# Attention and a routed expert layer in one program: routing sums in the accumulator's own bank, expert weights asked for before rows, pads written one at a time

## The chip, the cores and the metric

The program runs on one core of one Trainium2 chip. The metric is the device time in microseconds (us) of one execution; of several executions the median is taken. Five engines work side by side, each through its own instructions in order: PE (matmuls), DVE (vector work), ACT (activations), POOL (here mostly scatters by DMA) and SP (which issues most of the DMAs). They wait for each other through semaphores. PE writes its results into PSUM, eight banks of which this kernel uses all.

## What is computed

The reference has two halves. The first, for each of 8 batches of 2496 tokens with 256 channels:

```python
scores = scale * np.matmul(z, z.transpose(0, 2, 1))
attn = np.maximum(scores, 0.0) ** 2
out = np.matmul(attn, v)
return (u * out).astype(np.float32)
```

The second takes these 19968 rows x, and sends each row to the one of 8 experts with the largest logit:

```python
xn = x / (np.linalg.norm(x, axis=-1, keepdims=True) + 1e-06)
logits = xn @ en.T / tau
expert_idx = np.argmax(logits, axis=1)
...
h = np.maximum(x[mask] @ w1[e], 0.0)
out[mask] = gate_w[mask, None] * (h @ w2[e])
```

Here gate_w is the softmax value of the chosen expert.

## The kernel before, in words

**Attention.** Each batch is cut into 5 groups of up to 512 tokens, and each group runs over 20 steps of 128 tokens: 800 steps in all, one after the other. In a step PE computes a block of scores (L300, L301), ACT takes relu and square (L303, L307), DVE splits the square into a high and a low half in 16 bits (L314, L315), and PE multiplies the halves with the values into two accumulators, `acc[0]` and `acc[1]` (L344 to L346, in the last step of a group L341 and L342). Scores are symmetric, so a block below the diagonal is not computed again but taken from an earlier one, turned by DMA; steps that make their own block are called own steps here. Halves are made four own steps ahead of their use, scores five. In the first step of a group the matmuls into `acc[1]` are held back into the second step.

**PSUM.** Three banks hold scores (psS). Four hold accumulators (psA): two for the group at work, two for the group before it. One bank (psM, tile `pm`) is shared by everything small: the sum of squares of a group (`total`, L383), its logits (`logits`, L412), the ranks of its rows within the experts (`rank`, L496), and the scales of weights, z and v (L131, L147, L553, L571). While one user's result lies in `pm`, the next user waits. A flag, `state["pm"]`, and the third entry of a queue item keep the pieces of weight preparation from being started into an occupied `pm` (`pm_free`).

**Routing.** When a group's last step is done, `route` puts its pieces into a queue, each with the number of steps after which it is due: gate_x 0 (DVE: accumulators times u, L374), squares 4 (ACT, L378), total 7 (PE, L383), scale 9 (DVE, L391), high 11 (ACT, L398), low 13 (DVE, L401), turn 15 (SP, four turning DMAs, L406), logits 17 (PE), take 19 (DVE, L431, L432), top 20, rank 23 (PE), place 25 (DVE, L506 to L515: row positions, from `pm`), and from 34 to 48 the norm and the gates; scatters 49 (POOL, L521) write the rows into the table xs in DRAM, sorted by expert. The pieces of a group so run during the next two groups or so. Group numbers below count through all batches, from 0 to 39. The order of ACT, DVE and SP is that of the program text; PE and POOL are ordered by a planner of the framework, which can put a small matmul some steps later if it thinks its input late.

**Experts.** Rows are taken from xs in 61 tiles of 256 and 41 of 128 (slots). A slot loads rows (`slot_x`: a turning DMA, L890, and the gates, L891), weights (`slot_w`, up to 1 MB each, L904; from the fifth slot on only if the expert changes, L906), does the first layer (`slot_up`: tiles `ph` in psA, L923 to L925, relu on ACT L927, low half on DVE L928) and the second (`slot_down`, L947 to L949, DVE L953), and scatters the results (POOL, L954). Rows are asked for six slots ahead, weights four. The pieces still in the queue go on during the first slots: `pop` advances the step count by one after each tile. `slot_first` asks for the first slots' rows and weights during the last group, at step 789; it stands in SP's order behind the scatters of group 36. A read of xs waits for all scatters before it in the program, a scatter for the reads before it.

**Pads.** Behind the last row of each expert a block of 128 rows with an invalid index is written into xs (L861), at a position that SP reads from a table. All eight are written by one queue item, `pads`, due after the last group's scatters and the final table.

Of the kernel before, what the change touches and what calls it, by code (L numbers as in the profile page):

```python
# [7 lines left out]
F32 = mybir.dt.float32  # L8
F32R = mybir.dt.float32r
F16 = mybir.dt.float16  # L10
BF16 = mybir.dt.bfloat16
I32 = mybir.dt.int32
# [7 lines left out]
P = 128  # L20
# [8 lines left out]
TABLE = 36  # L29
NWB = 4  # L30
XFIRST, XAHEAD = 3, 6


def ceil_div(a, b):
    return -(-a // b)
# [10 lines left out]
def relu2_attention_then_moe(ctx, tc, zT, uT, v, emb, tau, w1, w2, ident, tri, iota_e, out):  # L46
    nc = tc.nc
    B, DQ, S = zT.shape
    D = uT.shape[1]
    E, _, F = w1.shape  # L50
# [25 lines left out]
    psM = ctx.enter_context(tc.tile_pool(name="psM", bufs=1, space=PSUM))  # L76
# [212 lines left out]
    state = {"pm": False}  # L289
# [66 lines left out]
    def route(b, g, acc, ut):  # L356

        t0, n = groups[g]
        nj = ceil_div(n, P)
# [10 lines left out]
        loc = {}  # L370
# [8 lines left out]
            loc["ssq"] = ssq  # L379

        def total():
            pm = psM.tile([P, 512], F32, name="pm", tag="m")
            nc.tensor.matmul(pm[:, 0:1], ones_b, loc["ssq"].bitcast(BF16)[:, 1:2], start=True, stop=True)  # L383
            loc["pm"] = pm
            state["pm"] = True

        def scale():
            pm = loc.pop("pm")
            state["pm"] = False
            h = rt.tile([P, 1], I32, name="h23", tag="h23")  # L390
            nc.vector.tensor_scalar(h, pm.bitcast(I32)[:, 0:1], 24, 23,  # L391
                                    op0=ALU.logical_shift_right, op1=ALU.logical_shift_left)
            up = rt.tile([P, 1], F32, name="up", tag="up")
            nc.vector.tensor_scalar(up.bitcast(I32), h, -1.0, float(198 << 23), op0=ALU.mult, op1=ALU.add)
            loc.update(h=h, up=up)
# [10 lines left out]
                nc.sync.dma_start_transpose(row16[:, 0:nj, q * P:(q + 1) * P], xhl[:, q, 0:nj * P])  # L406

        def logits():
            pm = psM.tile([P, 512], F32, name="pm", tag="m")
            for j in range(nj):  # L410
                for q in range(4):
                    nc.tensor.matmul(pm[:, j * 2 * E:(j + 1) * 2 * E], xhl[:, q, j * P:(j + 1) * P], enhl[:, q % 2, :],  # L412
                                     start=(q == 0), stop=(q == 3))
            loc["pm"] = pm
            state["pm"] = True

        def rest_scale():
            h, up = loc["h"], loc["up"]
# [6 lines left out]
            loc.update(odn=odn, epu=epu)  # L425

        def take():
            pm = loc.pop("pm")
            state["pm"] = False
            pv = pm[:, 0:nj * 2 * E].rearrange("p (j c) -> p j c", c=2 * E)  # L430
            nc.vector.tensor_copy(lg[:, :nj, :], pv[:, :, 0:E])  # L431
            nc.vector.tensor_tensor(lg[:, :nj, :], lg[:, :nj, :], pv[:, :, E:], op=ALU.add)  # L432
            m = rt.tile([P, 4], F32, name="m", tag="m")
            nc.vector.tensor_reduce(m[:, :nj], lg[:, :nj, :], axis=AX.X, op=ALU.max)
            sh = rt.tile([P, 4, E], F32, name="sh", tag="sh")
            nc.vector.tensor_tensor(sh[:, :nj, :], lg[:, :nj, :], m[:, :nj].unsqueeze(2).broadcast_to([P, nj, E]), op=ALU.subtract)
            loc["sh"] = sh
# [80 lines left out]
        def scatters():  # L518
            for j in range(nj):
# [2 lines left out]
                    xs[:, :], bass.IndirectOffsetOnAxis(ap=loc["dsti"][:m, j:j + 1], axis=0),  # L522
                    row[:m, j, 0:ROW], None)

        return [(0, gate_x), (4, squares), (7, total, True), (9, scale), (11, high), (13, low), (15, turn), (17, logits, True),
                (18, rest_scale), (19, take), (20, top), (23, rank, True), (25, place), (34, sums)] \
            + [(36 + j, norm(j)) for j in range(nj)] \
            + [(41, root), (42, roots), (43, shifted), (46, exps), (48, gates), (49, scatters)]
# [93 lines left out]
    steps = [(b, g, s) for b in range(B) for g in range(NG) for s in range(NST)]  # L622
# [42 lines left out]
    ones_b = cst.tile([P, P], BF16, name="ones_b")  # L665
# [58 lines left out]
    pm = psM.tile([P, 512], F32, name="pm", tag="m")  # L724
# [130 lines left out]
    nc.vector.memset(pad.bitcast(I32)[:, D + 1:D + 2], N)  # L855
    tails = cst.tile([1, E], I32, name="tails")

    def pads():
        for e in range(E):
            r = nc.sync.value_load(tails[0:1, e:e + 1], min_val=e * CAP, max_val=e * CAP + N)  # L860
            nc.sync.dma_start(xs[bass.ds(r, TB), :], pad[:TB])  # L861

    nc.sync.dma_start(xs[E * CAP:E * CAP + TB, :], pad[:TB])

# [2 lines left out]
    queue = []  # L867
# [9 lines left out]
    def slot_of(k):  # L877
        return (tables["A"], k, TA) if k < KA else (tables["B"], k - KA, TB)

    def slot_x(k):  # L880

        tab, i, T = slot_of(k)
        off = nc.sync.value_load(tab[0:1, 0, i:i + 1], min_val=0, max_val=E * CAP + TB - T)
        if k < XFIRST:
            xt = mx.tile([P, 4, T], F16, name="xt16", tag="xt16")
            me = mx.tile([P, T // P, ROW - D], F32, name="me", tag="me")
        else:
            xt = mst["mr"].tile([P, 4, T], F16, name="xr16", tag="xr16")
            me = mst["mr"].tile([P, T // P, ROW - D], F32, name="mer", tag="mer")
        nc.sync.dma_start_transpose(xt, xs[bass.ds(off, T), :].bitcast(F16)[:, 0:2 * D])  # L890
        nc.sync.dma_start(me, xs[bass.ds(off, T), D:ROW].rearrange("(j p) w -> p j w", p=P))  # L891
        mst["x", k] = xt, me

    def slot_w(k, i):
        tab, c, _ = slot_of(k)
        if i == 0:
            e = nc.sync.value_load(tab[0:1, 1, c:c + 1], min_val=0, max_val=E - 1)
            new = None if k < NWB else nc.sync.value_load(tab[0:1, 2, c:c + 1], min_val=0, max_val=1)
            mst["e", k] = e, new
        else:  # L900
            e, new = mst.pop(("e", k))
        src = wsd[bass.ds(e, 1), :, (0, WR1)[i]:(WR1, WR1 + WR2)[i]].rearrange("e p w -> (e p) w")
        if new is None:
            nc.sync.dma_start(mst["w"][i][k], src)  # L904
        else:
            nc.sync.dma_start(mst["w"][i][k % NWB], src, cond=new, cond_hint=False)  # L906
# [52 lines left out]
    def slot_first():  # L959

        mst["w"] = ([wp.tile([P, WR1], F16, name="wa0", tag="wr1"), wp.tile([P, WR1], F16, name="wa1", tag="wo")],
                    [wp.tile([P, WR2], F16, name="wb0", tag="wr2")])
        slot_x(0)
        slot_w(0, 0)
        slot_w(0, 1)
        slot_w(1, 0)
        for k in range(1, XFIRST):
            slot_x(k)

    def slot_pools():  # L970
# [48 lines left out]
    for i, (b, g, s) in enumerate(steps):  # L1019
# [49 lines left out]
        if i == len(steps) - 1 - NST // 2:  # L1069
            for f in follow:  # L1070
                if f is not None:
                    f()
            follow = []
            slot_weights()
            slot_first()
        if s == NST - 1:
            queue += [(i + p[0], p[1], len(p) > 2) for p in route(b, g, accs.pop((b, g)), uts.pop((b, g)))]
            if b == B - 2 and g == NG - 1:
                queue.append((i + TABLE, table_a, False))
            queue.sort(key=lambda x: x[0])  # L1080
            run(i)
        if own:
            if nd + LOOK - 1 < len(direct):
                st = direct[nd + LOOK - 1]
                halves[st] = parts(*st, probs.pop(st))
            nd += 1
    queue += [(len(steps) + TABLE, table_b, False), (len(steps) + TABLE, pads, False)]
    state["step"] = len(steps) - 1
    actx.close()
    slot_pools()  # L1090
# [102 lines left out]
```

## Time and profile before

| | us |
|---|---|
| median of 3 executions | 2218.98 (2212.02 to 2219.06) |
| the profiled execution | 2217.79 |
| its span, first to last instruction | 2215.6 |
| mean granted TensorE clock, share of full | 0.988 |
| PE busy | 2105.5 (95%) |
| DVE busy | 1421.2 (64%) |
| ACT busy | 1197.7 (54%) |
| POOL busy | 349.9 (16%) |

Attention lasts to about 1348 us of the span, the experts from there to the end. Times in the timeline are us from the span's start. "Idle before" is the time in which the engine had nothing to do before an instruction, and the arrow names what ended it; the releaser is inferred from semaphores. SPq is SP's queue of DMA issues: such a row tells when the DMA was issued, not when it landed.

### The profile page before, as it was taken

The page shows a single profiled execution, that of the slowest core. Times are in us where ns is not written, and L with a number is a line of the kernel's source. Part 1 is how long each engine was busy: PE and PEld are TensorE (multiplying, and loading weights), DVE is VectorE, ACT ScalarE, POOL GpSimd, SP SyncE. Part 2 cuts the span into 40 slices and gives each one's busy share as a digit, 9 for nine tenths or more (in the row PEclk, how much of TensorE's full clock was granted, in tenths as well). Part 3 has the DMA queues.
Part 4 walks back from the last instruction along what each step waited for, and adds up shares of the span by engine and source line. Part 5 has one row for each costly group of instructions (what it writes and reads, how often), then busy time and mean ns, then how long its engine had stood idle before and what let it go on. Part 6 is the DMA issues. An engine that isn't in the chain of part 4 may idle for free. (4 is left out here: it accounts for less than half of the span.)

```text
span 2215.6 us, 43233 instructions
## 1 busy us (share of the span) xinstructions
PE 2105.5 (95%) x15154; PEld 1345.1 (61%) x15154; DVE 1421.2 (64%) x3796; ACT 1197.7 (54%) x2329; POOL 349.9 (16%) x428
## 2 busy tenths in 40 slices
PE   6999899999999989999999998999999999999997
PEld 2444444444444434444444446888888888889996
DVE  7778878889888878788988864443333333333332
ACT  6768768768868758768868762222222222222221
POOL 0011111111111111111111111221111111111211
PEclk9999999999999999999999999999999999999999
DMA  6756957885975955967966646442233332237460
GB/s 167 174 129 186 203 149 183 189 209 137 209 195 140 234 138 132 248 151 185 207 178 148 138 98 204 112 122 62 56 89 87 91 93 49 50 101 196 107 165 27
DMA packets 610316, 317.85 MB, mean 143 GB/s; under 512 B 530981, under 2 KB 573486, under 8 KB 602928
## 3 DMA queue, kind: packets, MB, share of 16 engines
q1 hardware_dynamic: 594912, 273.82, 52.7%
q0 software_dynamic: 15184, 41.24, 5.8%
q8 instruction: 121, 1.98, 0.4%
q14 instruction: 99, 0.81, 0.1%
HBM read 297.95 MB, written 59.60 MB: 161 GB/s over the span
## 5 line engine op out<-in xcount | busy, mean ns | idle before, releaser
L303 ACT ACTIVATE a<-sc 128x512 f32<-128x512 f32 (+1 forms) x480 | 278.1, 580 | 109.3 <-PE sc L301 105.8
L307 ACT ACTIVATE a<-a 128x512 f32<-128x512 f32 (+1 forms) x480 | 300.6, 626 | 15.1
L346 PEld LDWEIGHTS <-vv 128*128 128x128 f16 x1520 | 149.4, 98 | 179.4 <-issue 11.2
L947 PE MATMUL po<-w,hh 128*128 128x256 f16 x944 | 257.3, 273 | 0.0
L949 PE MATMUL po<-w,hl 128*128 128x256 f16 x944 | 257.3, 273 | 0.0
L948 PE MATMUL po<-w,hh 128*128 128x256 f16 x944 | 257.3, 273 | 0.0
L344 PEld LDWEIGHTS <-vv 128*128 128x128 f16 x1520 | 149.3, 98 | 176.2 <-ACT vv L281 8.0
L521 POOL DMA_INDIRECT xs<-row,dsti x160 | 176.3, 1102 | 505.2 <-DMA xs<-row,dsti 296.2
L345 PEld LDWEIGHTS <-vv 128*128 128x128 f16 x1520 | 149.4, 98 | 164.5 <-issue 5.1
L954 POOL DMA_INDIRECT out_dram<-ot,mer x153 | 148.8, 972 | 608.8 <-DVE ot L953 374.5
L344 PE MATMUL acc<-tt,vv 128*128 128x512 f16 (+1 forms) x640 | 238.7, 373 | 1.1 <-DMA tt<-hl__372 1.1
L346 PE MATMUL acc<-tt,vv 128*128 128x512 f16 (+1 forms) x640 | 238.9, 373 | 0.0
L345 PE MATMUL acc<-tt,vv 128*128 128x512 f16 (+1 forms) x640 | 238.8, 373 | 0.0
L300 PE MATMUL sc<-z 128*128 128x512 f16 (+1 forms) x480 | 183.1, 382 | 11.6 <-ACT a L303 6.6
L953 DVE TENSOR_SCALAR ot<-po,mer,w 128x256 f32<-128x256 f32 x114 | 58.0, 541 | 200.1 <-PE po L949 194.8
L301 PE MATMUL sc<-z,z 128*128 128x512 f16 (+1 forms) x480 | 183.0, 381 | 0.0
L949 PEld LDWEIGHTS <-hl 128*128 128x128 f16 x1272 | 124.5, 98 | 14.5
L947 PEld LDWEIGHTS <-hh 128*128 128x128 f16 x1272 | 124.5, 98 | 13.9
L948 PEld LDWEIGHTS <-hh 128*128 128x128 f16 x1272 | 124.5, 98 | 13.9
L449 POOL MEMSET ob<- 128x72 bf16 x40 | 6.2, 158 | 664.7 <-DVE pos L511 645.9
L947 PE MATMUL po<-wb,hh 128*128 128x256 f16 x328 | 89.4, 273 | 0.0
L949 PE MATMUL po<-wb,hl 128*128 128x256 f16 x328 | 89.4, 273 | 0.0
(4162 smaller groups left out, 5148.1 us busy)
## 6 DMA issues: line engine op xcount, KB each, us to landing
w<-wsd SPq DMA_DIRECT2D x73, 1026.0 KB
wa<-wsd SPq DMA_DIRECT2D x50, 1024.0 KB
w<-wsd SPq DMA_DIRECT2D x48, 1024.0 KB
wb<-wsd SPq DMA_DIRECT2D x25, 1026.0 KB
scan<-in_v_dram SPq DMA_DIRECT2D x56, 312.0 KB
vt<-in_v_dram SPq DMA_DIRECT2D x133, 128.0 KB
ut<-in_uT_dram SPq DMA_DIRECT2D x32, 512.0 KB
wr<-in_w_dram SPq DMA_DIRECT2D x16, 1024.0 KB
```

The source lines that it names most:

```text
L300: nc.tensor.matmul(sc[:, :n], z1[:, ss], z1[:, t0:t0 + n], start=True, stop=False)
L301: nc.tensor.matmul(sc[:, :n], z1[:, ss], z2[:, t0:t0 + n], start=False, stop=True)
L303: nc.scalar.activation(a[:, :n], sc[:, :n], AF.Relu, scale=2.0 ** -SHIFT)
L307: nc.scalar.activation(a[:, :n], a[:, :n], AF.Square)
L344: nc.tensor.matmul(acc[k][:, :n], va, ph[:, :n], start=first, stop=False)
L345: nc.tensor.matmul(acc[k][:, :n], va, pl[:, :n], start=False, stop=False)
L346: nc.tensor.matmul(acc[k][:, :n], vb, ph[:, :n], start=False, stop=last)
L521: nc.gpsimd.indirect_dma_start(xs[:, :], bass.IndirectOffsetOnAxis(ap=loc["dsti"][:m, j:j + 1], axis=0), row[:m, j, 0:ROW], None)
L947: nc.tensor.matmul(o, hh[:, f, t], wh, start=(f == 0), stop=False)
L948: nc.tensor.matmul(o, hh[:, f, t], wl, start=False, stop=False)
L949: nc.tensor.matmul(o, hl[:, f, t], wh, start=False, stop=(f == NF - 1))
L954: nc.gpsimd.indirect_dma_start(out, bass.IndirectOffsetOnAxis(ap=me.bitcast(U32)[:, j, 1:2], axis=0), ot[:, j, :], None, bounds_check=N - ...
```

## The change

`total` and `logits` no longer take a tile of the shared bank. They write into `acc[1]` of their own group, whose contents `gate_x` has read by then; `scale` and `take` read from there. Their queue items lose the mark that keeps others out of `pm`. In `slot_first` the row load of the first slot moves behind the three first weight loads. The eight pads become eight queue items, due 18, 20, ... 32 steps after the table's due time in place of all at once.

```diff
--- before.py
+++ after.py
@@ -379,16 +379,11 @@
             loc["ssq"] = ssq
 
         def total():
-            pm = psM.tile([P, 512], F32, name="pm", tag="m")
-            nc.tensor.matmul(pm[:, 0:1], ones_b, loc["ssq"].bitcast(BF16)[:, 1:2], start=True, stop=True)
-            loc["pm"] = pm
-            state["pm"] = True
+            nc.tensor.matmul(acc[1][:, 0:1], ones_b, loc["ssq"].bitcast(BF16)[:, 1:2], start=True, stop=True)
 
         def scale():
-            pm = loc.pop("pm")
-            state["pm"] = False
             h = rt.tile([P, 1], I32, name="h23", tag="h23")
-            nc.vector.tensor_scalar(h, pm.bitcast(I32)[:, 0:1], 24, 23,
+            nc.vector.tensor_scalar(h, acc[1].bitcast(I32)[:, 0:1], 24, 23,
                                     op0=ALU.logical_shift_right, op1=ALU.logical_shift_left)
             up = rt.tile([P, 1], F32, name="up", tag="up")
             nc.vector.tensor_scalar(up.bitcast(I32), h, -1.0, float(198 << 23), op0=ALU.mult, op1=ALU.add)
@@ -406,13 +401,11 @@
                 nc.sync.dma_start_transpose(row16[:, 0:nj, q * P:(q + 1) * P], xhl[:, q, 0:nj * P])
 
         def logits():
-            pm = psM.tile([P, 512], F32, name="pm", tag="m")
+            pm = acc[1]
             for j in range(nj):
                 for q in range(4):
                     nc.tensor.matmul(pm[:, j * 2 * E:(j + 1) * 2 * E], xhl[:, q, j * P:(j + 1) * P], enhl[:, q % 2, :],
                                      start=(q == 0), stop=(q == 3))
-            loc["pm"] = pm
-            state["pm"] = True
 
         def rest_scale():
             h, up = loc["h"], loc["up"]
@@ -425,9 +418,7 @@
             loc.update(odn=odn, epu=epu)
 
         def take():
-            pm = loc.pop("pm")
-            state["pm"] = False
-            pv = pm[:, 0:nj * 2 * E].rearrange("p (j c) -> p j c", c=2 * E)
+            pv = acc[1][:, 0:nj * 2 * E].rearrange("p (j c) -> p j c", c=2 * E)
             nc.vector.tensor_copy(lg[:, :nj, :], pv[:, :, 0:E])
             nc.vector.tensor_tensor(lg[:, :nj, :], lg[:, :nj, :], pv[:, :, E:], op=ALU.add)
             m = rt.tile([P, 4], F32, name="m", tag="m")
@@ -522,7 +513,7 @@
                     xs[:, :], bass.IndirectOffsetOnAxis(ap=loc["dsti"][:m, j:j + 1], axis=0),
                     row[:m, j, 0:ROW], None)
 
-        return [(0, gate_x), (4, squares), (7, total, True), (9, scale), (11, high), (13, low), (15, turn), (17, logits, True),
+        return [(0, gate_x), (4, squares), (7, total), (9, scale), (11, high), (13, low), (15, turn), (17, logits),
                 (18, rest_scale), (19, take), (20, top), (23, rank, True), (25, place), (34, sums)] \
             + [(36 + j, norm(j)) for j in range(nj)] \
             + [(41, root), (42, roots), (43, shifted), (46, exps), (48, gates), (49, scatters)]
@@ -855,10 +846,11 @@
     nc.vector.memset(pad.bitcast(I32)[:, D + 1:D + 2], N)
     tails = cst.tile([1, E], I32, name="tails")
 
-    def pads():
-        for e in range(E):
+    def pads(e):
+        def f():
             r = nc.sync.value_load(tails[0:1, e:e + 1], min_val=e * CAP, max_val=e * CAP + N)
             nc.sync.dma_start(xs[bass.ds(r, TB), :], pad[:TB])
+        return f
 
     nc.sync.dma_start(xs[E * CAP:E * CAP + TB, :], pad[:TB])
 
@@ -960,11 +952,10 @@
 
         mst["w"] = ([wp.tile([P, WR1], F16, name="wa0", tag="wr1"), wp.tile([P, WR1], F16, name="wa1", tag="wo")],
                     [wp.tile([P, WR2], F16, name="wb0", tag="wr2")])
-        slot_x(0)
         slot_w(0, 0)
         slot_w(0, 1)
         slot_w(1, 0)
-        for k in range(1, XFIRST):
+        for k in range(XFIRST):
             slot_x(k)
 
     def slot_pools():
@@ -1084,7 +1075,7 @@
                 st = direct[nd + LOOK - 1]
                 halves[st] = parts(*st, probs.pop(st))
             nd += 1
-    queue += [(len(steps) + TABLE, table_b, False), (len(steps) + TABLE, pads, False)]
+    queue += [(len(steps) + TABLE, table_b, False), *[(len(steps) + TABLE + 18 + 2 * e, pads(e), False) for e in range(E)]]
     state["step"] = len(steps) - 1
     actx.close()
     slot_pools()
```

## Rows read from the trace of the kernel before

**Rows 1.** The page: span; busy time (us) of each engine.

```profile
span 2215.6 us, 43233 instructions
PE 2105.5 (95%) x15154; PEld 1345.1 (61%) x15154; DVE 1421.2 (64%) x3796; ACT 1197.7 (54%) x2329; POOL 349.9 (16%) x428
```

**Rows 2.** Windows: stretch, length, busy of PE, PEld, DVE, ACT, POOL; clock, DMA, GB/s.

```profile
60.00:1348.00 1288.00, 1223.53 (x6451) 568.15 (x6449) 1056.90 (x3087) 960.72 (x1910) 182.08 (x244) 0.99 0.72 171
1348.00:2204.00 856.00, 841.49 (x8548) 761.60 (x8547) 321.53 (x599) 195.40 (x340) 166.45 (x174) 0.99 0.39 103
...
80.00:120.00 40.00, 34.38 (x167) 15.05 (x166) 26.23 (x60) 20.67 (x36) 0.16 (x1) 0.91 0.85 193
1320.00:1360.00 40.00, 35.41 (x226) 19.99 (x224) 17.91 (x72) 11.26 (x29) 4.57 (x6) 0.91 0.45 130
1480.00:1520.00 40.00, 36.28 (x317) 31.91 (x318) 12.95 (x21) 8.10 (x14) 8.74 (x9) 0.96 0.42 107
```

**Rows 3.** Waits of PE, 60 to 1348 us: total us, times, longest us.

```profile
PE pm L383 <- DVE pos L511: 37.2, 15, 7.0
PE sc L300 <- ACT a L303: 6.6, 10, 1.5
PE pm L553 <- DVE lg L432: 2.6, 2, 1.9
```

**Rows 4.** Timeline of PE: start us, us, instruction, idle before it and releaser.

```profile
113.77 0.16 PE L383 MATMUL pm<-ssq,ones_b 128*128 128x1 bf16 x1 [5.62 <-DVE pos L511]
```

**Rows 5.** Timeline of DVE around the same instant.

```profile
112.65 0.80 DVE L114 TENSOR_REDUCE smxv<-scan 128x1 f32<-128x624 f32 x1 [6.65 <-DMA scan<-in_v_dram]
116.27 0.43 DVE L314 CAST hl__1093<-a 128x512 f16<-128x512 f32 x1
```

**Rows 6.** Timeline of PE, group 18: its sum, then its logits.

```profile
679.09 0.16 PE L383 MATMUL pm<-ssq,ones_b 128*128 128x1 bf16 x1 [2.48 <-DVE pos L511]
...
690.07 0.55 PE L412 MATMUL pm<-enhl,xhl 128*128 128x16 f16 x16
```

**Rows 7.** Timeline of DVE, group 18: the low halves for these logits.

```profile
688.16 1.28 DVE L401 SCALAR_TENSOR_TENSOR xhl<-xt,up,xhl 128x1024 f16<-128x1024 f32 x1
```

**Rows 8.** Timeline of PE: first matmul into the second accumulator, groups 22 and 25.

```profile
769.55 0.38 PE L344 MATMUL acc<-tt,vv 128*128 128x512 f16 x1
...
870.66 0.38 PE L344 MATMUL acc<-hl__10506,vv 128*128 128x512 f16 x1
```

**Rows 9.** Timeline of DVE: last read of the logits, groups 20 and 23.

```profile
765.29 0.19 DVE L432 TENSOR_TENSOR lg<-lg,pm 128x32 f32<-128x32 f32 x1
...
871.91 0.19 DVE L432 TENSOR_TENSOR lg<-lg,pm 128x32 f32<-128x32 f32 x1
```

**Rows 10.** Waits of SP's queue, whole span.

```profile
SPq L890 <- DMA xs<-row,dsti: 42.8, 3, 18.0
```

**Rows 11.** Timeline of SP's queue: first expert rows, first expert weights.

```profile
1344.86 1.27 SPq L890 DMA_TRANSPOSE xt<-xs  x1
...
1347.59 0.36 SPq L904 DMA_DIRECT2D wa<-wsd  x1
```

**Rows 12.** Waits of PE from 1348 us on.

```profile
PE ph__17184 L923 <- DMA wa<-wsd: 4.6, 1, 4.6
PE ph__19315 L923 <- DMA wa<-wsd: 3.8, 1, 3.8
```

**Rows 13.** Timeline of POOL: first scatter of group 36.

```profile
1332.68 0.97 POOL L521 DMA_INDIRECT xs<-row,dsti  x1 [1.76 <-DVE row L489]
```

**Rows 14.** Windows: the three first weight loads in flight.

```profile
1347.00:1359.00 12.00, 7.41 (x40) 4.94 (x38) 3.04 (x10) 1.19 (x2) 0.00 (x0) 0.72 0.96 307
```

**Rows 15.** Waits of POOL, whole span.

```profile
POOL xs L521 <- DMA xs<-row,dsti: 296.2, 106, 7.5
```

**Rows 16.** Timeline of SP's queue: the eight pads.

```profile
1473.63 8.25 SPq L861 DMA_DIRECT2D xs<-pad  x8
```

**Rows 17.** Timeline of ACT after the hand-over: the squares of group 39.

```profile
1366.17 0.95 ACT L378 ACTIVATE xhl<-xt 128x896 f16<-128x896 f32 x1 [4.50 <-DMA row<-xhl]
```

## The prediction

> **What bounds the kernel now.** I read the page first: PE is busy 2105.5 of 2215.6 us, so time can only come out of the 110 us in which it stands still, or out of its clock [rows 1]. The windows by stage say where that is: attention leaves PE idle for 1288.0 - 1223.5 = 64.5 us between 60 and 1348 us, the experts for 14.5 us of 856; the rest is start-up, which the change doesn't touch. In both stages the granted clock averages 0.99, and the short windows show where it falls: behind a wait of some us it drops from its upper level (2.4 GHz) to the lower one (1.2 GHz) for a while, which in a window of 40 us reads as 0.91 or 0.96, a loss of 3.6 or 1.6 us of work on top of the wait [rows 2]. Then the waits of PE: in attention one line holds more than half of the idle time, the sum of squares L383, 37.2 us in 15 waits, released by the previous group's `place` on DVE, which empties the shared bank. Waits on scores are 6.6 us; a transpose for the weights' scales, which waits for `take` to empty the bank, has 2.6 us [rows 3]. From 1348 us on two waits for weights are left, 4.6 and 3.8 us [rows 12].
>
> **Part 1, the accumulator's bank.** Nothing is added: the same matmuls and DVE reads go to another bank. Removed is the wait for `place`; the sum now waits only for its own input. Its worth lies between nothing (PE stands still a little later, for the same DVE) and 37.2 us plus some 10 us of clock. It has two kinds of waits.
>
> Two are long, 5.6 and 7.0 us together 12.6. In the first DVE is itself late: it stood 6.65 us for a scan's DMA, in front of `place`, and the next halves come out at 116.27 us, 2.5 us after PE was let go [rows 4, 5]. PE can bring forward only what was fed to it: I take two steps. A step is 1288/760 = 1.7 us, so 3.4 us for each, 7 in both.
>
> Thirteen are short, 24.6 us, 1.9 on average. Seven of them lie in the fourth group of a batch. In group 18 PE waited 2.48 us; ten us later its logits start at 690.07, and the low halves they need were ready at 688.16 + 1.28 = 689.44: only 0.6 us of the 2.48 can be kept, the rest becomes a wait for `low` [rows 6, 7]. I take 0.6 of each, 8 us. Of the waits of other small work on this bank I take 2 [rows 3].
>
> Added is a new wait. `acc[1]` comes free after `take`, 19 steps into the route, no longer after `gate_x` at 0, and the next user of the bank starts two groups on, some three steps behind `take`. Queued behind it on PE is everything; ACT, and DVE through it, wait for its scores. In the trace PE's first matmul into `acc[1]` of group 22 comes 4.1 us after the last read of group 20's logits; in group 25 it comes 1.4 us before group 23's [rows 8, 9]. Of 38 such pairs seven are short, by 3.9 us together, the rest have up to 5.4 us. I take 4 us. If DVE came later still this bound has no floor but the planner, which can put other matmuls first; as the lower end I take all that the edit saves and 9 more. Part 1: 7 + 8 + 2 - 4 = 13 us, between -9 and 50. The clock I leave at 0, because short waits stay where DVE is late.
>
> **Part 2, weights before rows.** SP stands 18.0 us at the first row load, until group 36's scatters have landed, and asks for the first weights 2.7 us after it; PE then waits 4.6 us for them, and its clock falls [rows 10, 11, 12, 2]. Moved are the row load's table read, turning DMA and gate DMA, past three weight loads of 1 MB on SP's queue. The weights need nothing that is late, so they are asked for at the place where SP now stands still. Rows of the first slot are then last. They can't come before 1344.86 plus their landing, and attention ends near 1348: the saving is between 0 and 4.6 + 3.6 = 8.2 us. The first of four scatters starts at 1332.68, while the weights would still be under way (three took most of the 12 us from 1347 on, with DMA 96% busy at 307 GB/s) [rows 13, 14]. A scatter waits for the one before it, 2.8 us as a rule (296.2 over 106) and 7.5 at worst [rows 15]. Two delayed by a good us each push the rows back by 3. I take 5 of the 8.2.
>
> The Trainium skill (DMA: Bandwidth & Descriptors, section Issuing engines are not separate DMA queues) says that DMAs of SP and POOL run on the same 16 engines and interleave, whoever issued them. By that the scatters do pay for the weights, which speaks against this part; the third rival below is what it would come to here. That scatters under load take up to 7.5 us agrees with it.
>
> Behind the first rows on SP stand the rows of slots 1 and 2 and then the four turning DMAs of group 38. With the weights out of the way they are issued some 3 us earlier, and the squares of group 39, which ACT does only at 1366.17 after 4.5 us of waiting for these DMAs, move forward with them [rows 17]. Against that `acc[1]` of the last group now stays taken through the first four slots, so the expert tiles turn over three banks instead of four. A bank comes free when DVE has read it; normally that is in time, but the fifth tile is held up by these squares, and the eighth would want its bank about 3 us early. I set the two against each other at 0, between -4 and +1.
>
> **Part 3, the pads.** SP writes eight in 8.25 us, one a us, and before that stands for the last scatters; the weights behind them are late and PE waits 3.8 us, then runs for a while at the lower clock, 1.6 us [rows 16, 12, 2]. After the change no pad stands before these weights. The next row load stops SP for the same scatters, but it is one slot later in the program, and rows are asked for six slots ahead, of 856/81.5 = 10.5 us each. Each pad still costs its table read and its DMA, about 1 us, and the wait for the row loads before it; the row load after it waits for its landing. Three pads come to one slot: some 3 us of issues and as much waiting, inside 10.5. What hides that is the lead of four slots for weights. Without it the 3.8 us would come back. I take 5 of 5.4, between 0 and 5.4.
>
> **The sum.** 13 + 5 + 0 + 5 = 23 us off the profiled execution of 2217.8, that is 2194.8. The median of the runs lies 1.2 us above that execution, so 2196.
>
> **Rivals.** First, DVE simply remains the feeder: every wait taken from the sum comes back at the logits, the halves or the new bank wait, and part 1 is worth 2 instead of 13. For it: group 18 above, and DVE is busy 1056.9 of 1288 us in attention. Against: DVE too stands still for 231 us there, partly for what a waiting PE has not made. Time 2207. Chance 0.20.
>
> Second, the buffer does its work: with more lead PE rides over DVE's late stretches, which is what a lead is for, and most of the 37.2 us and 5 us of clock go. Part 1 is then 35, the time 2174. Against it speak the short distances of rows 6 to 9. Chance 0.14.
>
> Third, the scatters pay in full: four at 2 us more each put the first rows back by 8, part 2 gives nothing, time 2201. Chance 0.12.
>
> Fourth, slower: the wait for `take` becomes the new stop of every group. It decides when DVE is later against PE than now by more than the distance of a pair, some 2 us on average. To lose 7 us over all, these waits must eat the 10 of parts 2 and 3 and 17 more, on top of the 37.2 that they replace: 54 us over 38 groups, 1.4 us each, as in group 25. Seven pairs are at or past that point now, and 31 are not. Time 2226. Chance 0.05.
>
> Fifth, the change doesn't do what it says: the sum waits just as long for its squares on ACT, or the planner places it as before, and the weights still come late. The releaser named in the rows is DVE's `place` in all 15 waits, so it has little. Time 2219. Chance 0.04.
>
> **The numbers.** My forecast has 0.45. About 0.3% of this kernel, 6.7 us, is what a measurement of it can tell from no change, so faster means under 2212.3. Forecast, second and third rival lie clear of it, the first near it, and I give a quarter of that to "same": 0.45 + 0.14 + 0.12 + 0.15 = 0.86, of which I move 0.05 to the others for what I have not seen. Faster 0.81, same 0.12, slower 0.07. The range reaches from the second rival, 2174, to the edge of the first, 2213.
>
> **What would show it.** Right: L383 gone from PE's waits on DVE in attention, a smaller wait at the logits (L412) or at the first matmuls into `acc` (L344, released by L432) in its place; the first weights asked for near 1327 us, and PE's first expert matmul released by the rows; no wait of PE near 1484 us and eight pads apart from each other on SP. PE's idle time between 60 and 1348 us should fall from 64.5 to about 50. Wrong: idle time there unchanged, with L344 named instead of L383, or the first rows landing 5 us or more later after the scatters.

## The result, and the profile after

The changed kernel takes 2195.06 us (median of four runs, 2193.44 to 2195.83) against 2219.02 for the kernel before (median of four, measured with it): ratio 0.9895, 95% interval 0.9871 to 0.992. Its profiled execution took 2194.44 us, 23.4 less than the profiled execution before. In the changed kernel the lines have moved up: the sum of squares is L382, the logits L407, `take`'s last read L423, `place` ends at L502, expert rows are L882, expert weights L896 and L898, pads L852, the first expert matmul L915.

The page, first its span and then the busy time of each engine, answers to [rows 1]:

```profile
span 2192.3 us, 43207 instructions
PE 2100.9 (96%) x15154; PEld 1345.3 (61%) x15154; DVE 1420.4 (65%) x3796; ACT 1196.4 (55%) x2329; POOL 352.5 (16%) x428
```

The work is the same. PE stands still for 2192.3 - 2100.9 = 91.4 us instead of 110.1, which is 18.7 of the 23.3 us; the other 4.6 are a shorter busy time for the same 15154 matmuls. The windows say from which stage. They answer to [rows 2]; those of 40 us are laid so that they hold the same two places, the hand-over and the pads:

```profile
60.00:1335.00 1275.00, 1222.49 (x6453) 569.48 (x6452) 1056.16 (x3087) 959.56 (x1911) 184.64 (x244) 0.99 0.74 175
1330.00:1370.00 40.00, 35.65 (x322) 29.35 (x320) 18.93 (x56) 10.38 (x21) 3.43 (x5) 0.96 0.79 202
1460.00:1500.00 40.00, 40.00 (x369) 35.84 (x368) 14.55 (x24) 9.55 (x16) 10.70 (x11) 1.00 0.38 97
```

Attention has 1275.00 - 1222.49 = 52.5 us of idle PE, 12.0 less than before. At the hand-over the granted clock averages 0.96 over 40 us where it was 0.91, and near the pads 1.00 where it was 0.96, without any idle time. The waits of PE in attention (total us, times, longest) answer to [rows 3]:

```profile
PE acc L382 <- ACT xhl L378: 10.7, 9, 2.2
PE sc L300 <- ACT a L303: 9.2, 12, 1.8
PE acc L407 <- DVE xhl L396: 5.3, 4, 1.7
PE pm L562 <- DVE pos L502: 3.8, 2, 3.5
PE pm L487 <- DVE wm L550: 3.3, 1, 3.3
...
PE pm L544 <- DVE sm1z L137: 2.4, 1, 2.4
PE acc L344 <- DVE lg L423: 2.2, 2, 1.4
```

The 37.2 us released by `place` are gone. The sum waits for its own squares on ScalarE instead (10.7), the logits for the low halves (5.3), the new bank wait is there (2.2), and the shared bank still stops PE for work of the weights and for rank: 3.8, 3.3 and 2.4. From the hand-over on PE's waits are these, where [rows 12] had 4.6 and 3.8:

```profile
PE ph__17106 L915 <- DMA xt<-xs: 2.8, 1, 2.8
PE ph__17295 L915 <- DVE hl L920: 1.0, 1, 1.0
PE acc L382 <- ACT xhl L378: 0.5, 1, 0.5
```

Before there were two more, below those of [rows 12] in the same view:

```profile
PE ph__18222 L923 <- DMA w<-wsd: 1.6, 1, 1.6
PE pm L383 <- DVE carry L509: 1.0, 1, 1.0
```

So the balance of the two profiled executions closes. Attention ends at 1334.80 instead of 1348.15 us: 13.35. The waits behind it are 4.3 instead of 11.0: 6.7. The lower clock costs (1 - 0.96) x 40 = 1.6 instead of 5.2 [rows 2]: 3.6, an estimate on the high side, since such a window also counts the lower clock while PE stands. Together 23.6 of 23.4.

**Where attention's 13 us come from.** I took the instant at which PE finishes each group, in both traces. The lead over the kernel before grows by 5.0 us from group 1 to 2 and by 7.4 from group 21 to 22, the places of the two long waits. All else together gives 1. This is one pair of executions; the section on the prediction sets more of them beside it. The first place, PE's timeline of the changed kernel beside [rows 4]:

```profile
109.49 0.16 PE L382 MATMUL acc<-ssq,ones_b 128*128 128x1 bf16 x1 [0.80 <-ACT xhl L378]
...
110.80 0.38 PE L300 MATMUL sc<-z 128*128 128x512 f16 x1
...
118.14 0.38 PE L344 MATMUL acc<-hl__1091,vv 128*128 128x512 f16 x1
```

and ScalarE's, before and then after (a fence for each kernel):

```profile
117.40 0.60 ACT L303 ACTIVATE a<-sc 128x512 f32<-128x512 f32 x1 [8.30 <-PE sc L301]
```

```profile
111.44 0.60 ACT L303 ACTIVATE a<-sc 128x512 f32<-128x512 f32 x1 [2.00 <-PE sc L301]
```

VectorE stands for the scan's DMA just as before (6.65 us, until 113.05). But PE goes on through four finished halves, and on the way makes scores for ScalarE, which starts again 6.0 us earlier. The matmul with the halves that VectorE makes first after its stop (`hl__1091`, `hl__1093` before) comes at 118.14 instead of 125.16.

Of these 7.0 us, 4.8 are the shorter stop. Most of the rest is the clock, which the prediction had left at 0 for this part. Behind its stops the kernel before ran at the lower level (1.2 GHz), as these windows show; the last but one column is the granted clock:

```profile
113.80:119.50 5.70, 5.70 (x15) 2.05 (x16) 3.65 (x10) 1.86 (x3) 0.16 (x1) 0.51 0.23 61
784.70:788.00 3.30, 3.30 (x10) 1.09 (x10) 3.09 (x13) 0.00 (x0) 0.92 (x2) 0.50 0.15 58
```

The changed kernel kept the upper level there:

```profile
109.50:118.00 8.50, 8.50 (x41) 3.90 (x41) 4.82 (x14) 5.42 (x9) 0.16 (x1) 1.00 0.49 152
```

At half pace the 5.7 and 3.3 us cost about 2.8 and 1.7 us (an estimate from these rows). Then 2.4 are lost again: at 127.29 us a transpose for the weights' scales (L544, in the list of waits above) stops PE, and over the whole group the lead grows by 5.0. The second place, PE before and PE after:

```profile
784.60 0.16 PE L383 MATMUL pm<-ssq,ones_b 128*128 128x1 bf16 x1 [7.00 <-DVE pos L511]
```

```profile
775.26 0.16 PE L382 MATMUL acc<-ssq,ones_b 128*128 128x1 bf16 x1 [1.38 <-ACT xhl L378]
```

**The hand-over.** SP's queue in the changed kernel, the three first weights and the first rows, answers to [rows 11]; below it POOL's first scatters of group 36, which answer to [rows 13]:

```profile
1313.26 0.37 SPq L896 DMA_DIRECT2D wa<-wsd  x1
1313.83 0.35 SPq L896 DMA_DIRECT2D wb<-wsd  x1
1315.00 0.34 SPq L896 DMA_DIRECT2D wa<-wsd  x1
1334.22 1.28 SPq L882 DMA_TRANSPOSE xt<-xs  x1
```

```profile
1319.35 0.97 POOL L512 DMA_INDIRECT xs<-row,dsti  x1 [1.76 <-DVE row L480]
1324.57 0.96 POOL L512 DMA_INDIRECT xs<-row,dsti  x1 [4.25 <-DMA xs<-row,dsti]
```

The weights are asked for where the prediction said (1327 less the 13 us by which all is earlier). They have landed some 11 us before attention ends: between 1324 and 1326 us the DMA engines move nothing. The rows come last. The first scatter pays for them: it took 4.95 us from issue to landing, 2.80 before. The rows are asked for 0.6 us before attention ends, where they were asked for 3.3 us before it.

**The pads.** The wait of 3.8 us near 1484 us was read as a wait for weights, because the profile names the load `wa<-wsd`. SP's queue before, and PE's first matmul after the wait, say otherwise:

```profile
1473.63 8.25 SPq L861 DMA_DIRECT2D xs<-pad  x8
1483.59 0.11 SPq L906 DMA_DIRECT2D wa<-wsd  x1
1484.05 0.35 SPq L906 DMA_DIRECT2D w<-wsd  x1
```

```profile
1483.72 0.28 PE L923 MATMUL ph__19315<-xr,wa 128*128 128x256 f16 x1 [3.77 <-DMA wa<-wsd]
```

PE goes on 0.13 us after SP has reached the load, far too soon for 1 MB: at the 307 GB/s of [rows 14] that would take about 3.4 us (an estimate). Its issue lasts 0.11 us, where that of a load which is carried out lasts 0.35. From the fifth slot on the kernel loads weights only if the expert changes, so this load was skipped, and PE waited for SP's turn behind the pads, not for data. The same 0.13 us stand in experiments 1, 2, 4 and 5. In the changed kernel SP passes this place 20 us before the first pad:

```profile
1442.60 0.08 SPq L898 DMA_DIRECT2D wa<-wsd  x1
...
1462.66 0.38 SPq L852 DMA_DIRECT2D xs<-pad  x1
```

### The profile page after: what moved, and what is told of

Same layout as the page of the kernel before. It is cut to its first block, busy times and chain, and to the rows that moved or that the text cites. A ratio compares the mean times of both kernels' runs of the same rounds, so it can differ in the third digit from the quotient of the medians.

```text
span 2192.3 us, 43207 instructions
## 1 busy us (share of the span) xinstructions
PE 2100.9 (96%) x15154; PEld 1345.3 (61%) x15154; DVE 1420.4 (65%) x3796; ACT 1196.4 (55%) x2329; POOL 352.5 (16%) x428
## 5 line engine op out<-in xcount | busy, mean ns | idle before, releaser
L939 PE MATMUL po<-wb,hh 128*128 128x256 f16 x328 | 89.4, 273 | 0.0
L940 PE MATMUL po<-wb,hh 128*128 128x256 f16 x328 | 89.4, 273 | 0.0
```

The source lines that it names most:

```text
L939: nc.tensor.matmul(o, hh[:, f, t], wh, start=(f == 0), stop=False)
L940: nc.tensor.matmul(o, hh[:, f, t], wl, start=False, stop=False)
```

## The experiments

All ratios are to the kernel before. Diffs are against it or against the changed kernel, as said.

**1. The bank's part alone.** The kernel before with the sum and the logits moved, as in the change:

```
-            nc.tensor.matmul(pm[:, 0:1], ones_b, loc["ssq"].bitcast(BF16)[:, 1:2], start=True, stop=True)
+            nc.tensor.matmul(acc[1][:, 0:1], ones_b, loc["ssq"].bitcast(BF16)[:, 1:2], start=True, stop=True)
...
-            pm = psM.tile([P, 512], F32, name="pm", tag="m")
+            pm = acc[1]
             for j in range(nj):
```

> Only part 1: total and logits of a group go into its own second accumulator bank; weights, rows and pads as before. Theory: the wait of the sum for the previous group's place is what attention loses, so the whole gain of attention is in this part. PE ends attention 13 us earlier than before (1348.1 to about 1335), and the time falls by 13 to 15 us; the two later waits of PE for weights (4.6 and 3.8 us) stay. Rival: DVE feeds PE, and the gain of attention needs something else of the change; then the time falls by 2 to 5 us and new waits of the same size stand at the logits or at the first matmuls into the accumulators.

Measured 0.9922 (0.9904 to 0.994), 17.3 us. Both waits named for weights stay, 4.6 and 3.9 us. In the profiled execution attention ended at 1339.56 us, 8.6 earlier than before and not 13; it was the slowest of the six (2208.53, median 2202.58).

**2. Weights before rows alone**, in the kernel before:

```
-        slot_x(0)
         slot_w(0, 0)
...
-        for k in range(1, XFIRST):
+        for k in range(XFIRST):
```

> Only part 2: the first three weight loads stand ahead of the first row load on SP. Theory: weights land long before PE needs them, the wait moves to the rows, which are 1 to 3 us later because the first scatter of group 36 runs beside the weights and takes about 5 us in place of 2.8; the time falls by 2 to 5 us. Rival: the rows are not late and the clock stays up; the time falls by 8 us. Second rival: the scatters pay in full; no change.

Measured 0.9987 (0.9974 to 1.0), 2.9 us; the interval reaches from 0 to 5.8, so it rules out the first rival's 8, but neither the 2 to 5 of the theory nor the second rival. PE's waits from the hand-over on:

```profile
PE pm L383 <- DVE pos L511: 4.5, 1, 4.5
PE ph__17184 L923 <- DMA xt<-xs: 1.1, 1, 1.1
PE ph__19315 L923 <- DMA wa<-wsd: 0.5, 1, 0.5
PE po L947 <- DMA w<-wsd: 0.4, 1, 0.4
```

The wait for weights at the hand-over has become 1.1 us for rows. PE, sooner at the sum of the last group, waits there for the shared bank, 4.5 us instead of 1.0. With the sum in its own bank that stop is 0.5 us in the changed kernel and 2.2 to 2.3 in experiments 8, 11 and 12, so that the two parts help each other here is likely but rests on one profile. The third row was not expected: the wait at the pads has fallen from 3.8 to 0.5 although the pads stand where they stood. Against the end of attention SP starts to write them 6.3 us earlier than before, and so it is also earlier at the load behind them. Parts 2 and 3 therefore share this wait, and their gains alone need not add.

**3. The pads alone**, in the kernel before:

```
-    queue += [(len(steps) + TABLE, table_b, False), (len(steps) + TABLE, pads, False)]
+    queue += [(len(steps) + TABLE, table_b, False), *[(len(steps) + TABLE + 18 + 2 * e, pads(e), False) for e in range(E)]]
```

> Only part 3: pads one by one, 18 to 32 steps later. Theory: the weights behind the pads are asked for before PE needs them; the wait of 3.8 us near 1484 us and the stretch at the lower clock behind it go, and the time falls by 5 us. Rival: the row load that follows stops SP for the same scatters, so a wait for weights comes back a slot later; no change.

Measured 0.9976 (0.9966 to 0.9986), 5.3 us; the wait of 3.8 us is gone.

**4 and 5. The sum alone, the logits alone**, in the kernel before: of the diff of experiment 1 the first pair of lines without the second, then the second without the first.

> A piece of part 1: only total moves into the accumulator's bank; logits stay in the shared bank and keep their mark. Theory: the 37.2 us of waits stood at the sum alone, so most of part 1 is here: the time falls by 9 to 13 us, and the bank is free after scale, so no matmul into the accumulators waits for take. Rival: sum and logits only help together, since other small work waits as long for take or for place as before; the time falls by less than 5 us.

Measured 0.9926 (0.9909 to 0.9942).

> The kernel before with only the logits in the group's own accumulator bank; the sum stays in the shared bank. Theory (the whole gain of the bank's part is the sum's; the sum alone gave 0.9926, sum and logits 0.9922): the 37 us of waits at the sum for place stay, and the ratio is 0.998 to 1.003. Rival (the logits free the bank for the sum and the weights as well, and one of the two moves is as good as the other): the waits at the sum shrink and the ratio is 0.993 to 0.996.

Measured 1.0004 (0.9992 to 1.0015). The sum's wait is still PE's largest:

```profile
PE pm L383 <- DVE pos L507: 32.0, 16, 5.5
```

The sum's move is the whole of the bank's gain; that of the logits is worth nothing that can be measured.

**6. Asking earlier**, in the changed kernel:

```
-        if i == len(steps) - 1 - NST // 2:
+        if i == len(steps) - 1 - NST // 2 - 6:
```

> The changed kernel with the first expert weights, and behind them on SP the first row loads, asked six steps earlier: at step 783, ahead of the scatters of group 36 (step 788) instead of just behind. Theory (after the change the expert part starts late because the first row load is issued only when the last of group 36's scatters has landed: 1334.22 us, landed 1337.5, PE idle 2.77 there and half clock for 3.4 us behind it): the rows then wait only for group 35's scatters, PE's wait for rows at the first expert step goes, the wait of 1.0 for the eighth tile's halves goes as well, and the time falls by about 4 us against the changed kernel, to about 2191 (0.9875 of the kernel before). Rival: rows asked earlier delay the scatters and the turns queued behind them on SP, the wait moves to another tile and the time stays at 2195 (0.9895).

Measured 0.9863 (0.9838 to 0.9887), about 7 us below the changed kernel's 0.9895. PE has no wait left from the hand-over on. Two rows show the price, SP's first row load and POOL's first scatter of group 36:

```profile
1314.15 4.09 SPq L882 DMA_TRANSPOSE xt<-xs  x1
```

```profile
1327.96 0.97 POOL L512 DMA_INDIRECT xs<-row,dsti  x1 [12.06 <-DMA me<-xs]
```

The row load now holds the queue for 4.09 us and the scatters stand for 12 us behind the reads, but nobody needs them soon. Of the 7 us, the waits and the lower clock at the hand-over make up 4.3 + 1.6. The gain repeats: from attention's end to the end of the span it takes 851.5 us here, 851.8 and 851.0 in experiments 9 and 10, against 857.5 in the changed kernel and 857.4 to 860.3 in experiments 7, 8, 11 and 12. The rest is no more than what two executions of the same attention differ by.

**7. Sum and logits due one step later**, in the changed kernel:

```
-        return [(0, gate_x), (4, squares), (7, total), (9, scale), (11, high), (13, low), (15, turn), (17, logits),
+        return [(0, gate_x), (4, squares), (8, total), (9, scale), (11, high), (13, low), (15, turn), (18, logits),
```

> The changed kernel with the matmul of the sum due at step 8 of a group instead of 7, and that of the logits at 18 instead of 17. Theory (what is left of the wait at the sum, 10.7 us in 9 waits, is the sum asked before ScalarE has squared the next group, and 5.3 us in 4 waits the logits asked before VectorE has the low half): a step later these two waits shrink to under 5 us together and the time falls by up to 8 us, to about 2187 to 2195 (0.986 to 0.9895). Rival: the waits at the sum come where PE has run out of finished halves, so a later total only moves the wait to the score or value matmuls, and VectorE gets its scale a step later: PE idles as long and the time stays at 2195, or rises by 1 to 3 us.

Measured 0.9897 (0.9875 to 0.9919): the rival. The waits moved, as these rows beside those of the changed kernel above show:

```profile
PE sc L300 <- ACT a L303: 16.4, 15, 3.6
...
PE acc L407 <- DVE xhl L396: 2.7, 4, 1.0
PE acc L382 <- ACT xhl L378: 2.3, 4, 0.8
```

The squares' wait fell by 8.4 us, that for `a`, the scores after relu, rose by 7.2. ScalarE squares the rows as well as it makes `a`; where PE waits for it is only the name of the wait.

**8. The shared bank kept clear around rank**, in the changed kernel:

```
         def place():
             ob, pm = loc["ob"], loc.pop("pm")
-            state["pm"] = False
...
-                (18, rest_scale), (19, take), (20, top), (23, rank, True), (25, place), (34, sums)] \
+                (18, rest_scale), (19, take), (20, top), (23, rank, True), (25, place), (29, lambda: state.update(pm=False)), (34, sums)] \
...
-        return not state["pm"] and not any(takes and due <= i + 1 for due, _, takes in queue)
+        return not state["pm"] and not any(takes and due <= i + 4 for due, _, takes in queue)
```

> The changed kernel with the shared bank kept free of the weights' small work for longer around the rank of a group: the flag stays set from rank to step 29 instead of to place (25), and small work that needs the bank isn't started within four steps ahead of rank instead of one. Theory (the short waits were not gained because other users of the shared bank took the place of the sum: the powers' matmul waiting 3.5 us for place at 277.04, rank waiting for a copy out at 407.59, each with a stretch at half clock behind it): these waits go, PE idles some 8 to 10 us less in attention and the time falls by 5 to 10 us, to about 2185 to 2190 (0.985 to 0.987). Rival: with these waits gone VectorE's halves are late by the same amount, the wait moves to the score or value matmuls and the time stays at 2195 within 3 us; or the small work is pushed past the end of attention and the time rises.

Measured 0.9938 (0.9918 to 0.9958): 10 us slower than the changed kernel. The two targeted waits went, yet PE idles more in attention (the window from 60 us to its end), and two waits have grown:

```profile
60.00:1341.00 1281.00, 1224.77 (x6454) 569.58 (x6453) 1057.53 (x3088) 958.24 (x1911) 180.54 (x244) 0.99 0.73 174
```

```profile
PE acc L382 <- ACT xhl L378: 18.0, 9, 3.2
...
PE acc L344 <- DVE lg L423: 6.4, 7, 2.1
```

1281.00 - 1224.77 = 56.2 us of idle time against 52.5, which is 3.7 of the 10 us; where the others go was not followed. The waits for squares and for `take` grow by 7.3 + 4.2, more than the 6.9 that the two were worth. Which of the delayed steps pushes the squares back was not followed, so the cause of that growth stays open.

**9. The edits of 6 and 8 in one kernel.**

> Both of the above edits in one kernel: weights and rows asked six steps earlier, and the shared bank kept free for longer around rank. If both theories hold, the two gains add: about 2181 to 2186 (0.983 to 0.985). If only the earlier asking pays, 2191; if only the longer guard, 2185 to 2190; if neither, 2195.

Measured 0.9901 (0.9879 to 0.9924): the earlier asking pays here too (0.0037), the guard costs here too.

**10. The version that the parts suggest**: experiment 6 with the logits back in the shared bank.

```
-            pm = acc[1]
+            pm = psM.tile([P, 512], F32, name="pm", tag="m")
             for j in range(nj):
...
-        return [(0, gate_x), (4, squares), (7, total), (9, scale), (11, high), (13, low), (15, turn), (17, logits),
+        return [(0, gate_x), (4, squares), (7, total), (9, scale), (11, high), (13, low), (15, turn), (17, logits, True),
```

> The changed kernel with the logits put back into the shared bank, and weights and rows asked six steps earlier. Theory (the logits' move is worth nothing, the earlier asking about 7 us): the same time as the changed kernel asked earlier, 2188 (0.986), within 3 us. Rival (the weights' small work, which must then make room for the logits again, pushes the sum's gain away): 2192 or more (0.988).

Measured 0.9852 (0.9838 to 0.9866), 2184.49 us. It is clearly below the changed kernel and equal to experiment 6 within the intervals: again the logits' move has no worth.

**11 and 12. What removes the pads' wait.** The changed kernel with all pads at once, but late, and with the pads spaced, but early:

```
-(len(steps) + TABLE + 18 + 2 * e, pads(e), False)
+(len(steps) + TABLE + 18, pads(e), False)
```

```
-(len(steps) + TABLE + 18 + 2 * e, pads(e), False)
+(len(steps) + TABLE + 2 * e, pads(e), False)
```

> The changed kernel with all eight pads together at the new, later place (step +18), not two steps apart. Theory (being late is enough, since the weights for the first two experts are already asked by then, and the eight pads' 12 us on SP then delay only what is due much later): no wait of TensorE for weights near 1460 to 1490 and 2195 within 3 us. Rival (spacing is what matters): a wait of 3 to 5 us for the next weights on TensorE, about 2200.

Measured 0.989 (0.9876 to 0.9904), no wait for weights; the eight pads held SP for 8.18 us.

> The changed kernel with the pads one by one, two steps apart, but from the old place on, 18 steps earlier. Theory (either of being late and being spaced removes the wait): no wait of TensorE for weights, and 2195 within 3 us. Rival (only being late matters): TensorE waits 3 to 5 us for weights at the second expert's tiles, about 2200.

Measured 0.992 (0.9906 to 0.9935), with a wait of 1.7 us for second-layer weights, a load that was carried out and had been issued behind the pads. SP's queue shows that the spacing was lost:

```profile
1451.85 7.14 SPq L852 DMA_DIRECT2D xs<-pad  x7
```

SP had stopped for the last scatters, and everything due in the meantime went out in a row behind them. So being late is enough. The wait of 1.7 is smaller than the 5 us that this kernel loses to experiment 11. Its four runs spread over 8 us and the profiled one, 2194.55, is the fastest and shows no loss, so the cause of the 5 us stays open. The changed kernel with all pads together at the old place was not run; experiment 12 comes nearest to it.

## Why the prediction came out

**The time.** 2196 was forecast, 2195.06 measured. In the one pair of profiled executions the parts come out at 13.35 for attention (forecast 13 for part 1) and 10.3 behind it (forecast 5 + 0 + 5), but within attention at 12.4 for the two long waits and 1 for all else (forecast 7 and 8 + 2 - 4 = 6). Other profiles show that this split is an accident of the pair. Experiments 2 and 3 run the attention of the kernel before, experiments 1, 6, 11 and 12 that of the changed kernel (6 differs in the last group only). All in us, lowest to highest:

| | before, exp. 2, 3 | changed, exp. 1, 6, 11, 12 | difference of means | forecast |
|---|---|---|---|---|
| end of attention | 1348.2 to 1351.1 | 1333.1 to 1339.6 | 14.3 | 13 |
| groups 2 and 22, with the long waits | 78.2 to 81.1 | 68.7 to 73.6 | 8.1 | 7 |
| all else up to there | 1267.1 to 1272.5 | 1259.9 to 1268.3 | 6.2 | 6 |
| PE idle, from 60 us to there | 62.1 to 64.5 | 48.8 to 52.6 | 12.2 | about 14 |

Behind attention the kernels with the old hand-over and pads (before, experiments 1, 4, 5) take 866.7 to 870.0 us, those with the new (changed, 7, 8, 11, 12) 857.4 to 860.3: 9.6 between the means, forecast 10. So the terms of the sum came out near their forecasts, and the sum with them; some of the reasons did not. Of the 14.3 us of attention, 12.2 are idle time and the rest a shorter busy time for the same matmuls: the clock, left at 0, gave some 2 us.

**The long waits, forecast 7.** The reason given, "PE can bring forward only what was fed to it: I take two steps", doesn't hold. I read the next halves at 116.27 us [rows 5] as the limit, but four older ones lay finished, PE used them up at full pace, and its scores for the following steps feed ScalarE while VectorE stands. At 125 us of the kernel before the lead was 7.0, not 3.4. That two steps are nearly what is left at the end of the group, 3.4 on average at the first place and 4.7 at the second, is luck: the clock gave more and the stop at L544, 2.3 to 2.5 us in all five profiles, took some back. The clock is also what the profiles differ in. In experiments 1, 6, 11 and 12 it falls to the lower level behind that stop, in the changed kernel's own profile it doesn't; in experiments 6 and 12 it falls at the second place too. Against the one profile of the kernel before, the two places give 12.4 in the changed kernel, 9.8, 7.8, 10.6 and 7.5 in those four, and 12.4, 10.7, 10.9, 7.7 and 12.2 in experiments 4 and 7 to 10.

**The short waits, forecast 8 + 2 - 4.** "I take 0.6 of each" was right in direction and, with the other two terms, near in size: all else gave 6.2 on average. In single profiles it is anything from -1 to 7, so no one of them can size this term. What took the rest I had seen only in part: the low halves (L407, 5.3 us). The largest is the sum's own input, the squares on ScalarE, 10.7 us, which I had not priced at all. Experiment 7 shows that these waits are ScalarE's and VectorE's pace under several names.

**The bank's new wait, forecast 4,** measured 2.2, in two places; the fourth rival (every group stopped there) needed it in 38. Its price is real, though: in experiment 8 it grew to 6.4.

**Part 2, forecast 5.** The rows were to be pushed back by 3: they are asked for 2.7 us later against attention's end. PE's wait fell from 4.6 to 2.8, the lower clock's cost there from 3.6 to 1.6, the last sum's wait from 1.0 to 0.5: 4.3 in all. The Trainium skill's rule that transfers issued by different engines run on the same 16 DMA engines and interleave (DMA: Bandwidth & Descriptors, section Issuing engines are not separate DMA queues) is borne out by the first scatter, 4.95 us instead of 2.80, and 4.5 to 4.7 in experiments 2, 11 and 12. The third rival asked for four such scatters, and the next three landed in 2.5 to 4.1. Alone the part measured 2.9 within 0 to 5.8, so the forecast of 5 stands there too. What I had not seen is that it takes most of part 3's wait with it (experiment 2).

**Three banks instead of four, forecast 0 within -4 to +1.** The eighth tile waits 1.0 us for its bank, as described. The squares that hold up the fifth came forward by the 3 us that were said: they start 10.6 us behind the first expert matmul instead of 13.4 [rows 17].

```profile
1348.13 0.95 ACT L378 ACTIVATE xhl<-xt 128x896 f16<-128x896 f32 x1 [2.74 <-DMA row<-xhl]
```

**Part 3, forecast 5 of 5.4.** Alone it gave 5.3. That the pads stood ahead of what PE waited for was right, and experiment 11 shows that moving them behind it is enough. That "the weights behind them are late" was wrong: the load was skipped, and SP's turn was late. Parts 1, 2 and 3 alone add to 17.3 + 2.9 + 5.3 = 25.5, together they gave 24.0; what part 3 is worth beside part 2 no run shows cleanly. The 5 us of experiment 12 say that it is worth its 5, the 0.5 us left in experiment 2 that it is worth little.

**The rivals.** The first (VectorE remains the feeder) is true of most of the short waits and of experiment 7, but not of the long ones. The second (35 us from the buffer) needed the halves to be ready everywhere. Of the fifth, the sum does wait for its squares, but 10.7 us and not 37.2.

## What to carry to other kernels

A long stop of one engine behind a shared buffer can give back its whole length and its clock when the stopped engine has finished input in store, and what it does meanwhile restarts others; the next stop behind it then takes a part. Short stops at the pace of a feeder mostly change their names, whichever matmul is scheduled later: about a quarter came back here. Before sizing such a wait, count what lies finished in front of it, and list every input of the waiting instruction, not only the one that the trace names. A load named as the releaser need not have moved anything: look at how soon after its issue the waiting engine went on. Compare terms of a few us over several profiles of the same code, since the clock falls behind a stop in one and not in another. Where an engine stops for one transfer, look at which requests in its queue don't need it: moving these ahead of the stop gave about 3 and 7 us here (experiments 2 and 6). Spacing requests out gave nothing over asking for them together, later (experiment 11).

## What the runs showed of the hardware

A turning DMA issued right behind three weight loads held SP's queue for 4.09 us, the next one 2.36, the third 1.25 (experiment 6); issued with the weights landed it took 1.28. A queue's issue time is thus no constant. In the same kernel the first scatter of group 36 stood 12.06 us for reads of the table that they write. The issue of a weight load that the kernel skips lasted 0.07 to 0.11 us, that of one carried out 0.34 to 0.38, and PE went on 0.13 us after the issue of a skipped one (kernel before, experiments 1, 2, 4 and 5).
